# Layer two's short last blocks, loads in the arms of missing blocks, and an accumulator for the third block

## The chip, the core and the metric

The kernel runs on one core of a Trainium2 chip. The time is the device time of one execution in microseconds; three runs of the kernel before took 1007.67, 1007.77 and 1010.33 us, the median is 1007.77. The engines are TensorE (matrix products), VectorE, ScalarE, GpSimd and SyncE (SP), which issues most DMAs. In the profile PE is TensorE's products, PEld its weight loads, DVE is VectorE, ACT is ScalarE, POOL is GpSimd.

## The reference

Attention over 4 x 8 heads of 576 x 64, in which each query keeps its 32 best keys, gives 2304 tokens of 512 values. Two mixture layers of 8 experts follow. Each sends a token to the one expert that its gate rates highest; the second computes only tokens whose skip score is positive and adds its result to the token.

```python
for e in range(E):                      # layer two; xc are the tokens with x @ w_skip > 0
    mask = e_idx == e
    h = np.maximum(xc[mask] @ w1[e], 0.0)          # [rows, 512] @ [512, 1024]
    y[mask] = gate_w[mask, None] * (h @ w2[e])     # [rows, 1024] @ [1024, 512]
out[do_compute] = xc + y
```

With the inputs timed, layer one's experts get 416, 213, 291, 369, 216, 215, 285 and 299 rows, layer two's 177, 156, 141, 117, 320, 314, 175 and 143.

## The kernel before

The attention fills the first 480 us and scatters each token's row into its expert's stretch of a table in DRAM. Then come 16 experts, eight a layer, one after the other, with their order of work written out by hand (the program is scheduled as it is written). Every engine takes its instructions in that order.

Numbers are kept as pairs: a value is split into a high half (rounded to the format that TensorE multiplies at full pace, F32R) and a low half (the rest). A product is then high x high, high x low and low x high. Weights come by DMA into one of eight raw buffers (`fetch`); `split` (L779) lets ScalarE copy the high half and GpSimd or VectorE subtract it for the low one, and then fetches the raw data of eight pieces later. `post.lo` (`LO`) says which of an expert's eight pieces VectorE subtracts: 1, 3 and 5 in layer two. VectorE's `one_port` (L82) is an elementwise operation that also accumulates into a spare column.

An expert (`expert`, L879) does this:

- `xT` (L822): the tokens, up to `BLOCKS` blocks of 128 rows (four in layer one, three in layer two), are transposed by TensorE and split. The first two blocks always run; `optional` (L807) puts the others inside `If`s on the number of rows.
- For each f of 0 to 7, `mm1` (L832) multiplies the first weights by all tokens at once, 12 products into one of three accumulators H. Two nested `If`s on TensorE choose the smallest of four widths that holds the rows: (192, 256, 320, 384) in layer two. ScalarE and VectorE make h's halves from it, 384 columns wide. In between the weights of this expert's second product and the next expert's first are split.
- `mm2` (L861) multiplies h of a block of 128 rows by the second weights: 24 products of 512 columns into an accumulator, eight f by three pairs. First the third and fourth blocks, inside `If`s, then block 1 into Y[1], then block 0 into Y[0]; of block 0 the last three f come after the next expert's transposes. A third block takes Y[0], a fourth one of H.
- `post` makes a block's result. `later` gives its further steps: in layer two the scatter to the output, in layer one also transposes (`turn`), products (`logits`) and counts (`places`) on TensorE that route the token in layer two. `tick` (L873) runs one waiting step of each open block at fixed points between products; those of a third or fourth block again inside `If`s (L932).

An `If` whose arm isn't taken leaves an engine's semaphore behind those of the taken arm. The program then makes it up at the join: the engine's sequencer waits until the engine has done all its instructions, and adds what is missing. In the profile these are EVENT_SEMAPHORE rows of line 813.

The wait that the third block's accumulator brings follows from the order: the products of block 0 write Y[0], and so come behind the third block's read of it on VectorE, also where that block is missing and VectorE only makes up its count.

Of the kernel before, what the change touches and what calls it, by code (L numbers as in the profile page):

```python
# [540 lines left out]
WIDTHS = ((224, 304, 416, 512), (192, 256, 320, 384))  # L541
# [191 lines left out]
class Moe:  # L733
# [9 lines left out]
    def open(self, sb, psum, posts):  # L743
# [5 lines left out]
        self.HT = [sb.tile([128, 2, 512], F32R, name="h%d" % i) for i in range(8)]  # L749
# [48 lines left out]
    def counts(self, e):  # L798

        why = "a count of rows; it is only compared"  # L800
        at = self.ns[0:1, 9 + e:10 + e]
        nc = self.tc.nc
        self.n[e] = (nc.values_load(at, min_val=0, max_val=2304, skip_runtime_bounds_check_because=why),
                     nc.values_load(at, engines=[mybir.EngineType.PE], min_val=0, max_val=2304,
                                    skip_runtime_bounds_check_because=why))

    def optional(self, g, fn, rising=False):  # L807

        n = self.n[g % 8][0]

        def some(j):
            if j < BLOCKS[g // 8]:
                with self.tc.If(n > 128 * j):  # L813
                    if rising:
                        fn(j)
                    some(j + 1)
                    if not rising:
                        fn(j)

        some(2)  # L820
# [51 lines left out]

    def tick(self):  # L873

        for steps in self.open_rows:
            steps.pop(0)()
        self.open_rows = [r for r in self.open_rows if r]

    def expert(self, g):  # L879
# [9 lines left out]
        self.optional(g, lambda j: self.xT(g, j), True)  # L889
# [16 lines left out]
        for f in range(8):  # L906
            self.mm1(g, f)
            for i in range(4):
# [8 lines left out]
            if f == 4 and nxt:  # L917
                self.counts(e + 1)
        if g == 15:
            self.tc.nc.gpsimd.drain()  # L920
        while first:
            first.pop(0)()
        steps = {}

        def block(j):
            p = self.H[(8 * g + 8) % 3] if j == 3 else self.Y[0]
# [4 lines left out]
        late = max(len(t) for t in steps.values())  # L931
        self.open_rows.append([lambda i=i: self.optional(g, lambda j: steps[j][i]())  # L932
                               for i in ((0, 2, 5) if late > 1 else (0,))])
# [11 lines left out]
    def layer(self, layer, ns):  # L945
        tc, nc = self.tc, self.tc.nc
        g0 = layer * 8
        self.ns, self.n, self.open_rows = ns, {}, []
# [7 lines left out]
        self.counts(0)  # L956
# [161 lines left out]
def attention_moe_kernel(ctx: ExitStack, tc, q, k, v, wg1, w11, w12, wskip, wg2, w21, w22, out):  # L1118
# [23 lines left out]
    for bp in range(NP):  # L1142
        nc.gpsimd.iota(ev.tok[:, bp * 9:bp * 9 + 8], pattern=[[S, 2], [128, 4]], base=2 * bp * S, channel_multiplier=1,
                       allow_small_or_imprecise_dtypes=True)
        for b in range(2):
            nc.gpsimd.iota(ev.tok[b * 64:b * 64 + 64, bp * 9 + 8:bp * 9 + 9], pattern=[[0, 1]],
                           base=(2 * bp + b) * S + 512, channel_multiplier=1, allow_small_or_imprecise_dtypes=True)
    ev.wrong = consts.tile([128, 3], F32, name="wrong")
# [101 lines left out]
```

## Time and profile before

| | us |
|---|---|
| median of three runs | 1007.77 |
| the profiled execution | 1005.58 |
| its span, first to last instruction | 1003.8 |
| TensorE's products busy in the span | 875.3 |
| VectorE, ScalarE, GpSimd busy | 719.7, 672.6, 631.8 |
| layer one's first product starts at | 482.7 |
| layer two's first transposes start at | 783.9 |

The profile is of one execution. Busy time is the union of an engine's instructions; products overlap one another in the records, so that the distance between two starts is the better price of one. "Idle before" is the time in which an engine had nothing running, with what released it.

### The profile page before, as it was taken

To read this page: it belongs to the slowest core of one execution; us is meant where nothing else is said; L and a number is where in the kernel's file an instruction comes from. 1 tells how busy PE (TensorE), PEld (TensorE's weight loads), DVE (VectorE), ACT (ScalarE), POOL (GpSimd) and SP (SyncE) were. 2 spreads that over 40 slices of the span, in tenths; PEclk is the share of its full clock that TensorE was granted. 3 is DMA by queue.
4 is the path that set the end of the run, shared out by engine and by line. 5 is a ranking of instruction groups with operands and counts; after the bars stand their busy time and mean duration, and the time that the engine had idled before them with its cause. 6 is when DMAs were issued, how large, how long until landed. Compare 5 with 4: busy or idle time off the path is not lost. (4 is left out here: it accounts for less than half of the span.)

```text
span 1003.8 us, 20600 instructions
## 1 busy us (share of the span) xinstructions
PE 875.3 (87%) x6343; PEld 695.5 (69%) x6343; DVE 719.7 (72%) x3411; ACT 672.6 (67%) x1342; POOL 631.8 (63%) x446
## 2 busy tenths in 40 slices
PE   7678888778778878778999999999998899999997
PEld 5355555455545555556988988887887788889886
DVE  7999999999999999997336634644563456654362
ACT  6699999999989999984535534555452444443342
POOL 6878878877879999853226435444543666654464
PEclk9599999999999999999999999999999999999999
DMA  6897010010202000002836534555533566665530
GB/s 227 262 314 238 24 49 25 3 71 2 72 1 93 13 33 32 2 1 97 287 114 214 175 132 150 176 191 192 168 121 99 185 209 213 219 197 163 183 115 27
DMA packets 55033, 127.72 MB, mean 127 GB/s; under 512 B 8105, under 2 KB 8105, under 8 KB 54864
## 3 DMA queue, kind: packets, MB, share of 16 engines
q1 hardware_dynamic: 46208, 107.64, 33.4%
q0 software_dynamic: 6400, 12.65, 3.3%
q10 hardware_dynamic: 2256, 5.25, 1.5%
q8 instruction: 97, 1.59, 0.7%
q14 instruction: 72, 0.59, 0.2%
HBM read 96.04 MB, written 37.86 MB: 133 GB/s over the span
## 5 line engine op out<-in xcount | busy, mean ns | idle before, releaser
L788 POOL TENSOR_TENSOR w<-raw,w 128x1024 fp32r<-128x1024 f32 x72 | 174.7, 2439 | 185.5 <-ACT w L786 116.6
L867 PE MATMUL y<-w,h 128*128 128x512 f32 x936 | 228.4, 396 | 10.6 <-PEq L813 4.1
L240 POOL TENSOR_TENSOR y<-s,sg 128x576 f32<-128x576 f32 x144 | 204.3, 1440 | 41.8 <-ACT sg L237 32.6
L843 PE MATMUL hp<-xT,w 128*128 128x192 f32 (+4 forms) x1536 | 212.2, 296 | 3.3 <-DVE h L858 2.4
L867 PEld LDWEIGHTS y<-w,h 128*128 128x128 f32 x936 | 171.4, 188 | 53.6 <-issue 13.7
L843 PEld LDWEIGHTS hp<-xT,w 128*128 128x128 f32 x1536 | 203.3, 190 | 6.3 <-DVE h L858 3.8
L209 DVE MAX8 ca<-s 128x8 f32<-128x82 f32 (+1 forms) x1008 | 154.2, 228 | 4.8 <-ACT s L198 4.8
L286 POOL TENSOR_TENSOR r<-s,r 128x576 f32<-128x576 f32 x96 | 135.9, 1429 | 19.4 <-DVE r L282 15.1
L858 DVE SCALAR_TENSOR_TENSOR h<-hp,h 128x512 fp32r<-128x512 f32 (+1 forms) x128 | 77.9, 621 | 79.8 <-ACT h L857 79.7
L857 ACT ACTIVATE h<-hp 128x512 fp32r<-128x512 f32 (+1 forms) x128 | 69.8, 545 | 93.5 <-PE hp L843 87.3
L786 ACT ACTIVATE w<-raw 128x1024 fp32r<-128x1024 f32 x126 | 131.4, 1054 | 0.9 <-POOL w L788 0.5
L322 PE MATMUL m<-ident,p 128*128 128x128 f32 x576 | 95.2, 292 | 29.7 <-DVE whole L362 11.2
L788 DVE TENSOR_TENSOR w<-raw,w 128x1024 fp32r<-128x1024 f32 x54 | 99.3, 1839 | 24.5 <-ACTq L813 15.2
L237 ACT ACTIVATE sg<-s,tm 128x576 f32<-128x576 f32 x144 | 112.0, 797 | 6.5 <-POOL tm L228 5.9
L322 PEld LDWEIGHTS m<-ident,p 128*128 128x128 f32 x576 | 64.7, 145 | 68.9 <-ACT p L294 21.6
L247 DVE MAX8 my<-y 128x8 f32<-128x576 f32 x144 | 101.9, 747 | 2.3 <-POOL y L240 2.3
L109 PE MATMUL s<-kT,qT 64*128 64x288 f32 x512 | 84.4, 448 | 15.2 <-ACT s L198 7.5
L198 ACT ACTIVATE s<-s 128x1152 f32<-128x1152 f32 (+1 forms) x73 | 81.5, 1118 | 12.1 <-PE s L109 9.6
L150 PE MATMUL m<-pT,v 128*64 128x128 f32 (+1 forms) x1280 | 85.5, 277 | 0.7 <-ACT oT L339 0.4
L328 ACT ACTIVATE pT<-m 128x512 f32<-128x512 f32 x144 | 80.5, 609 | 5.6 <-PE m L322 5.6
L294 ACT ACTIVATE p<-r,neg 128x576 f32<-128x576 f32 x96 | 75.4, 787 | 6.8 <-POOL r L286 6.4
L630 POOL DMA_INDIRECT out_dram<-yo,ix x40 | 50.0, 1249 | 41.8 <-DVE yo L1110 24.1
(166 smaller groups left out, 1217.3 us busy)
## 6 DMA issues: line engine op xcount, KB each, us to landing
raw<-in_moe_w_dram SPq DMA_DIRECT2D x119, 512.0 KB, 4.5
x<-zrow SPq DMA_DIRECT2D x16, 1028.0 KB, 18.8
xg<-x SPq DMA_DIRECT2D x50, 257.0 KB, 3.6
v<-in_v_dram SPq DMA_DIRECT2D x8, 576.0 KB, 4.0
kT<-in_k_dram SPq DMA_DIRECT2D x7, 576.0 KB, 3.9
qT<-in_q_dram SPq DMA_DIRECT2D x7, 576.0 KB, 4.8
raw<-in_moe_w_dram ACTq DMA_DIRECT2D x7, 512.0 KB, 6.4
xg<-x ACTq DMA_DIRECT2D x6, 257.0 KB, 4.9
```

Source lines behind the costliest of these rows:

```text
L109: nc.tensor.matmul(p[:, c, :288], d["qT"][h, b, t * 128:t * 128 + 128], d["kT"][h, b, cs], start=True, stop=True)
L150: nc.tensor.matmul(po[i * 64:i * 64 + 64, cs], d["vt"][:, b, i, c] if c < 4 else d["v8"][i * 64:i * 64 + 64, b], pts[i][:, c, cs] if c < 4 ...
L209: nc.vector.max(out=ca[:, c], in_=e["s"][hh][:, cut[c]:cut[c + 1]])
L237: nc.scalar.activation(sg, e["s"][hh], AF.Sign, bias=bt["tm"][:, w:w + 1], scale=-ONE_BELOW, accum_out=bt["ac"][:, w:w + 1])
L240: nc.gpsimd.tensor_mul(y, e["s"][hh], sg)
L247: nc.vector.max(out=bt["my"][:, 2 * i + hh, 8:], in_=e["y"][hh])
L286: nc.gpsimd.tensor_tensor(r, e["s"][hh], r, op=OP.subtract)
L322: nc.tensor.transpose(pp[:, c], e["p"][:, hh, c * 128:c * 128 + 128], ident)
L786: nc.scalar.activation(t[:, 0], raw, AF.Copy)
L788: eng.tensor_tensor(t[:, 1], raw, t[:, 0].bitcast(F32), op=OP.subtract)
L843: nc.tensor.matmul(p[:, :W], self.w1(g, c)[:, a, fs], x[:, c, b, :W], start=(i == 0), stop=(i == 11))
L867: nc.tensor.matmul(p, self.HT[f][:, a, js], self.W2[f // 2][:, b, f % 2 * 512:f % 2 * 512 + 512], start=(f + a + b == 0), stop=(f == 7 and ...
```

## The change

In layer two, mm1's widths become three: 192, 320, 384. All eight h tiles are now slices of two larger ones. VectorE also loads an expert's number of rows into a register.

`beside`: after f = 3 and f = 7 of the first product, if the last block of the expert has at most 64 rows, VectorE copies the low half of h of these rows into the 64 columns behind their high half, for four f at once. One load of 128 columns then carries both halves of such a block.

`seconds` takes the place of the loop over `mm2` in layer two. `mm2s` does a block's high half against both halves of the weights, in an order that leaves f = 4 to 7 against the low weights for last; then an `If` on TensorE: a full block does these four and the eight of h's low half; a short block does these four, each cut into two of 256 columns (the last on 64 rows), and four products of 16 columns with zeros. ScalarE copies the lower 64 rows of the accumulator into `low`. `finish` adds them to the upper 64 rows by a product with a shifted identity (`down`), or, where the block is full or missing, loads a weight of zeros. Block 1 is finished after two f of block 0, a third block at the tick in the middle of block 1.

A third block gets an accumulator of H, in both layers. And in the arms of missing blocks TensorE loads 16 columns of ones as many times as the taken arm has products: with the transposes (4 a block, both layers) and layer one's later steps (4, 4 and 2 a block).

```diff
-WIDTHS = ((224, 304, 416, 512), (192, 256, 320, 384))
+WIDTHS = ((224, 304, 416, 512), (192, 320, 384))
...
-        self.HT = [sb.tile([128, 2, 512], F32R, name="h%d" % i) for i in range(8)]
+        self.HH = [sb.tile([128, 4, 2, 512], F32R, name="h%d" % i) for i in range(2)]
+        self.HT = [h[:, i] for h in self.HH for i in range(4)]
+        self.low = [sb.tile([128, 512], F32R, name="low%d" % i) for i in range(2)]
...
+        if layer:
+            self.short[e] = nc.values_load(at, engines=[mybir.EngineType.DVE], min_val=0, max_val=2304,
+                                           skip_runtime_bounds_check_because=why)
+    def beside(self, e, half):
+        n, h = self.short[e], self.HH[half]
+        def move(j):
+            at = 128 * j
+            one_port(self.tc, self.ev, h[:, :, 0, at + 64:at + 128], h[:, :, 1, at:at + 64].bitcast(F32), 1.0, OP.mult)
+        with self.tc.If(n <= 192) as c:
+            move(1)
+        with c.Else():
+            with self.tc.If(n > 256):
+                with self.tc.If(n <= 320):
+                    move(2)
-    def optional(self, g, fn, rising=False):
+    def optional(self, g, fn, rising=False, products=0):
...
-                with self.tc.If(n > 128 * j):
+                with self.tc.If(n > 128 * j) as c:
...
+                if products:
+                    with c.Else():
+                        for i in range(products * (BLOCKS[g // 8] - j)):
+                            self.tc.nc.tensor.ldweights(self.ev.ones[:, :16])
...
+    def part(self, e, j):
+        return self.H[(8 * e + 9) % 3] if j == 2 else self.Y[j]
+    def mm2s(self, e, j, fs=range(8), ticks=True):
...
+        def product(f, a, b, last, rows=slice(0, 128), cut=1):
+            for i in range(cut):
+                c = slice(i * 512 // cut, (i + 1) * 512 // cut)
+                nc.tensor.matmul(p[rows, c], self.HT[f][:, a, js][:, rows],
+                                 self.W2[f // 2][:, b, f % 2 * 512 + c.start:f % 2 * 512 + c.stop],
+                                 start=(f + a + b == 0), stop=last)
+        for f in fs:
+            for b in range(2 if f < 4 else 1):
+                product(f, 0, b, False)
+            if ticks and f == 3:
+                self.tick()
+        with self.tc.If(self.n[e][1] > 128 * j + 64) as c:
+            for f in range(4, 8):
+                product(f, 0, 1, False)
+            for f in fs:
+                product(f, 1, 0, f == 7)
+        with c.Else():
+            for f in range(4, 8):
+                product(f, 0, 1, False, slice(0, 128 if f < 7 else 64), 2)
+            for i in range(4):
+                nc.tensor.matmul(p[64:, :16], self.ev.none, self.ev.ones[:, :16], start=False, stop=i == 3)
+        nc.scalar.activation(self.low[j % 2][64:], p[64:], AF.Copy)
+        if ticks:
+            self.tick()
+        return p
+    def finish(self, e, j):
+        pe, n, p = self.tc.nc.tensor, self.n[e][1], self.part(e, j)
+        def add():
+            pe.matmul(p[:64], self.ev.down[64:], self.low[j % 2][64:], start=False, stop=True)
+        with self.tc.If(n > 128 * j + 64) as c:
+            pe.ldweights(self.ev.none)
+        with c.Else():
+            if j == 1:
+                add()
...
+    def seconds(self, g):
+        e, post, steps = g % 8, self.posts[1], {}
+        def block(j):
+            self.mm2s(e, j, ticks=False)
+            steps[j] = post.later(g, j)
+        self.optional(g, block)
+        self.open_rows.append([lambda: (self.finish(e, 2), self.optional(
+            g, lambda j: (post(g, j, self.XG[g % 2][j], self.part(e, j)), steps[j][0]())))])
+        self.split(8 * g + 10, post.lo)
+        self.mm2s(e, 1)
+        self.split(8 * g + 11, post.lo)
+        self.mm2(0, range(2), False)
+        self.finish(e, 1)
+        post(g, 1, self.XG[g % 2][1], self.Y[1])
+        self.open_rows.append(post.later(g, 1))
+        self.mm2(0, range(2, HF if e < 7 else 8))
...
-        self.optional(g, lambda j: self.xT(g, j), True)
+        self.optional(g, lambda j: self.xT(g, j), True, 4)
...
+            if layer and f % 4 == 3:
+                self.beside(e, f // 4)
...
+        if layer:
+            return self.seconds(g)
...
-            p = self.H[(8 * g + 8) % 3] if j == 3 else self.Y[0]
+            p = self.H[(8 * g + 11 - j) % 3]
...
-        late = max(len(t) for t in steps.values())
-        self.open_rows.append([lambda i=i: self.optional(g, lambda j: steps[j][i]())
-                               for i in ((0, 2, 5) if late > 1 else (0,))])
+        self.open_rows.append([lambda i=i, n=n: self.optional(g, lambda j: steps[j][i](), products=n)
+                               for i, n in ((0, 4), (2, 4), (5, 2))])
```

## Rows read from the trace of the kernel before

**Rows 1.** The page: busy us by engine; GpSimd's busy tenths in 40 slices.

```profile
PE 875.3 (87%) x6343; PEld 695.5 (69%) x6343; DVE 719.7 (72%) x3411; ACT 672.6 (67%) x1342; POOL 631.8 (63%) x446
...
POOL 6878878877879999853226435444543666654464
```

**Rows 2.** Busy time by engine in two stretches: layer one, layer two.

```profile
core 0: us, PE busy (x) PEld busy (x) DVE busy (x) ACT busy (x) POOL busy (x), PEclk, DMA share, GB/s
526.00:783.00 257.00, 243.56 (x1498) 212.53 (x1498) 129.74 (x452) 124.70 (x207) 121.00 (x71) 0.99 0.49 161
...
783.00:998.00 215.00, 205.94 (x1278) 182.35 (x1278) 111.83 (x142) 95.28 (x142) 120.91 (x55) 1.00 0.54 172
```

**Rows 3.** TensorE's timeline, layer two: start, length, line, operation, count [idle before].

```profile
858.10 1.04 PE L827 MATMUL m<-ident,xg 128*128 128x128 f32 x8
...
861.45 6.84 PE L843 MATMUL hp<-xT,w 128*128 128x192 f32 x60
...
872.91 5.70 PE L867 MATMUL y<-w,h 128*128 128x512 f32 x24
879.52 3.71 PE L867 MATMUL y<-w,h 128*128 128x512 f32 x15 [0.91 <-DVEq L813]
883.06 1.48 PE L827 MATMUL m<-ident,xg 128*128 128x128 f32 x12
...
886.44 14.24 PE L843 MATMUL hp<-xT,w 128*128 128x320 f32 x96
900.51 14.47 PE L867 MATMUL y<-w,h 128*128 128x512 f32 x63
```

**Rows 4.** Line 813 from 526 us: TensorE's sequencer events, length in ns.

```profile
L813 PEldq EVENT_SEMAPHORE  x46: 51/51/51, 542.4 to 986.3; - x46
```

**Rows 5.** TensorE's timeline, layer one: second, third and eighth expert.

```profile
542.51 2.99 PE L867 MATMUL y<-w,h 128*128 128x512 f32 x12
545.64 2.98 PE L867 MATMUL y<-w,h 128*128 128x512 f32 x12
...
553.22 1.47 PE L827 MATMUL m<-ident,xg 128*128 128x128 f32 x12
555.12 2.34 PE L867 MATMUL y<-w,h 128*128 128x512 f32 x9 [0.42 <-PEq L813]
...
759.38 3.00 PE L867 MATMUL y<-w,h 128*128 128x512 f32 x12
762.68 1.03 PE L1070 MATMUL m<-wgt,yT 128*128 128x9 f32 x8 [0.30 <-PEq L813]
```

**Rows 6.** TensorE's timeline, layer one: a pair of small products.

```profile
740.59 0.18 PE L610 MATMUL m<-ob,tri 128*128 128x8 bf16 x1
740.62 0.17 PE L611 MATMUL m<-ob,ones 128*128 128x8 bf16 x1
```

**Rows 7.** Timeline of the other engines in layer two, fourth expert's second product.

```profile
868.85 9.46 POOL L788 TENSOR_TENSOR w<-raw,w 128x1024 fp32r<-128x1024 f32 x4
...
873.18 2.96 ACT L786 ACTIVATE w<-raw 128x1024 fp32r<-128x1024 f32 x3
...
874.27 5.14 DVE L788 TENSOR_TENSOR w<-raw,w 128x1024 fp32r<-128x1024 f32 x1 [0.39 <-ACT w L786]
...
880.55 1.22 DVE L788 TENSOR_TENSOR w<-raw,w 128x1024 fp32r<-128x1024 f32 x1
```

**Rows 8.** Line 84 (`one_port`): length in ns, least, median and most.

```profile
L84 DVE TENSOR_SCALAR_CACHE_REDUCE kb<-kths x24: 153/160/163, 34.1 to 451.7; 128x6 f32<-128x6 f32 x24
```

**Rows 9.** Groups by line and form: busy us, mean ns of one.

```profile
L282 DVE TENSOR_SCALAR r<-s,kths 128x576 f32<-128x576 f32 x43 | 26.8, 624 | 0.0
...
L1065 ACT ACTIVATE yT<-m 128x512 f32<-128x512 f32 x22 | 13.0, 596 | 31.6 <-PE m L1064 31.6
```

**Rows 10.** TensorE's waits, 783 to 1004 us: total us, times, longest.

```profile
PE y L867 <- DVEq L813: 2.1, 3, 0.9
...
PE y L867 <- PEq L813: 1.5, 3, 1.2
...
PE y L867 <- issue: 1.2, 1, 1.2
```

## What I predicted

> **What bounds the kernel now.** I read the page first: TensorE is busy 87% of the span [rows 1]. The busy time by stage says more. From 526 to 783 us (layer one after its first expert) TensorE's products take 243.6 of 257 us, from 783 to 998 (layer two) 205.9 of 215, at a granted clock of 0.99 and 1.00, that is 2.4 GHz; no other engine is over 57% there, and DMA is at about half [rows 2]. So both layers are a row of products on TensorE, and the change is worth what it takes off that row. TensorE's timeline gives the prices. Products of 512 columns: 63 take 14.47 us and 24 take 5.70, so (14.47-5.70)/39 = 0.225 us apiece. Products of 320 columns (the row from 886.44): 14.24/96 = 0.148; of 192: 6.84/60 = 0.114 [rows 3]. From 512 to 320 that is 0.0004 us a column, but 192 columns lie above that line, so there the weight load in front of each product sets the pace, at about 0.11.
>
> **Missing blocks' arms.** Where a block is missing, TensorE's sequencer makes up its semaphore count with an event that waits until all products are done; there are 46 of these from 526 us on [rows 4]. Twelve products should take 2.70 us; with such an arm between them the next one starts 3.13 us after the first (0.43 late), and where the arm is followed by another block's transposes or logits 3.30 us (0.60 late) [rows 5]. In layer one seven of eight experts lack a block, and each has three such arms behind its tokens' steps: 7 x (0.43+0.43+0.60) = 10.2 us. The arm in front of the first product: with all three blocks of layer two there, 12 transposes and 9 products take 886.44-883.06 = 3.38 us, with a block missing 8 transposes and the 9 take 861.45-858.10 = 3.35 [rows 3]; four transposes at 0.11 are 0.43, so the arm costs 0.40. In layer one with one block missing, 12 transposes (1.32) are followed by the product only after 1.90: 0.58 [rows 5]. Three experts at 0.40 and four at 0.58 make 3.5, six of layer two 2.4. Gross: 16.1 us in 34 arms. The arms around the blocks' own products stay.
>
> What stands there instead is 164 loads of 16 columns: layer one 40 with the transposes and 100 with the steps, layer two 24. The trace has no such load alone. The nearest: two loads of 128 bf16 columns, each with a product of 8 columns, start 0.03 us apart [rows 6]. I take 0.03 a load, and 0.11 an arm for the next large load, which then stands in the open: 0.23 for four, 0.35 for eight, 0.17 for two. That is 4 x 0.63 + 3 x 0.93 for the steps, 4 x 0.23 + 3 x 0.35 for layer one's transposes, 6 x 0.23 in layer two: 8.7 us. **Net: 7.4 off.** Bounds: nothing, if all of it lies in the shadow of the running product (16.1 off); and 0.11 a load as for a large one, with 0.11 an arm: 164 x 0.11 + 34 x 0.11 = 21.8, which is 5.7 lost. I stay near the pair, the only small loads in the trace.
>
> On this the Trainium skill has a price (TensorE: Matmul & The Clock Gate, section "LDWEIGHTS (loading the stationary operand)"): a load takes its columns over 1.2 ns, whatever the rows. For 16 columns that would be an estimate of 0.013 us, 2.1 us for all in place of 4.9, and the forecast 2.8 lower (the next large load's 0.11 left as it is). No row here shows a load of 16 columns.
>
> **Short last block.** All eight experts of layer two have a last block of at most 64 rows (177, 156, 141, 117, 320, 314, 175 and 143 rows), so each takes the short arm once. Before: 24 products of 512 columns, 5.40. After: 12 of these (2.70), 8 of 256 columns (0.122 by the slope above: 0.98), four of 16 columns with a weight of zeros (as the small pairs, 0.12 and 0.11 behind them), and later one product of 512 columns that adds the lower half (0.225): 4.13. Saved 1.27, **eight times: 10.2.** The branch is new, but the first product's branches, two ahead of each group of 12, cost nothing that its row of 60 products shows (6.84/60, the pace of the loads). Each expert also runs one load in place of an addition it doesn't need: 8 x 0.14 = 1.1 lost.
>
> What the short block adds off TensorE: ScalarE copies half a bank per block (512 columns out of PSUM take it 0.60 [rows 9]). The copy waits for TensorE behind two splits, and the third split behind it moves from 2.2 to about 4.9 us after the block's start at 872.91; all three are over 3.2 after that start now [rows 7]. Behind that split stand VectorE's half of it and the block's result: done near 8.6 after the start, just ahead of the next tokens' transposed rows. The fetch that the split issues on SP goes 3 us later; its data are used an expert later. The addition comes six products (1.35) after the block, the copy is done about 0.8 after it: hidden with 0.5 to spare; with ScalarE late, TensorE waits for the difference. VectorE gets two moves of 256 elements an expert. By the row of 576 elements in 0.62 us that is 0.28 [rows 9], and by the 6-element row of the same operation with accumulator 0.16 [rows 8] and the other 250 elements at that pace 0.43; 0.3 to 0.5 with the accumulator's read. The first lies between two results of the first product, whose buffers have a group of products to spare. The second ends about 1.7 us after the last group of the first product; TensorE wants it after eight products, 1.8. I take 0.06 a block for a late one, 0.5 lost, between nothing and 0.3 a block. Queued behind the move is VectorE's split, for which TensorE doesn't wait before the next expert.
>
> **Third block's accumulator.** The products of the first block, which come last, wait for VectorE now: the missing third block would have used their accumulator, and VectorE gets to that arm only after a split that took 5.14 us instead of 1.22 [rows 7]: the next 15 products start at 879.52 instead of 878.31, 1.21 late of which 0.91 is idle [rows 3]. There are three such waits, 2.1 us idle [rows 10], and with about 0.3 of restart each 3.0. With its own buffer nothing there waits for that arm; the first group of the next expert uses this buffer some 10 us later. **3.0 off**; nothing, if another wait for the same queue takes its place. Beside it stand two single stalls of 1.2 at the same place in the first two experts, put down to TensorE's own sequencer and to issue [rows 10]. Their cause isn't shown; I count half: 1.2 (between 0 and 2.4).
>
> **Three widths.** The eight experts take 192 or 320 columns before and after, so the products stay. One branch fewer in 48 groups: nothing, since none of these branches shows in the row. In layer one the third block's other buffer frees nothing that a row shows.
>
> **Sum:** 7.4 + 10.2 - 1.1 - 0.5 + 3.0 + 1.2 = 20.2 us. Of the profiled execution's 1005.58 (span 1003.8 and 1.8 around it) 985.4 remain; the median of the runs, 1007.77, is 2.2 above that execution, so I forecast **987.5**.
>
> **The rivals.** *Loads as dear as the drain.* If a small load costs what a large one does, the arms lose 5.7 instead of gaining 7.4: 1001. For it: no load of theirs has a product to hide behind; against it: the pair 0.03 apart [rows 6]. *Loads hidden.* The other bound: 8.7 less, 979. For it: products of 512 columns go at 0.225, their own length, so the load of each lies beside the product before [rows 3]; against it: only one load can lie there for each product. *The wait moves.* TensorE still waits for VectorE's arm, or for ScalarE's copy of the half bank: the 4.2 of the accumulator are gone and 0.5 an expert is added: 996. For it: VectorE's split stays where it is, and ScalarE's order now has a wait for TensorE in it.
>
> *Slower: the moves wait for GpSimd.* VectorE's split of two SBUF inputs took 5.14 instead of 1.22 while GpSimd ran four splits without a gap, 9.46 us from 868.85 [rows 7]. If the moves are held in the same way, the first one keeps the later results back until two of these are over (4.8 us, of which 3.5 reach TensorE after its spare group), and the second holds the short block's fifth group for up to 4: 7 us in each of the six experts of two blocks, 42 in all, so 987.5 + 42 = 1029. It turns the sign from 20.2/6 = 3.4 us an expert on. Against it: 24 operations of this very form, in a stage where GpSimd is busy six to nine tenths, never took over 0.163 [rows 1, 8]. The Trainium skill has this as a rule (SBUF — State Buffer, section "SBUF: two separate sides"): VectorE and GpSimd share a port pair under an exclusive lock, taken by VectorE's two-port modes and its operations with two SBUF inputs. The split agrees with it, 5.14; the moves have one input and an accumulator, and by the rule would wait only if they ran in such a mode.
>
> **Chances.** The forecast 56% (982 to 992), loads dear 13%, loads hidden 13%, the wait moved 11%, the moves held 4%, and 3% that these gains are eaten by something I don't see. The range goes from 977 to 999: the hidden loads with the two single stalls gone below, most of the dear loads above. A measurement here tells 0.3%, 3 us, from no change. Only the held moves and half of the unseen end above that: faster 0.92, same 0.03, slower 0.05.
>
> **What would show it.** The events in TensorE's sequencer fall from 46 to about 13. The packs of 12 products with an arm between start about 2.9 apart. A short block, up to the next product, takes near 3.9 in place of 5.4, and an expert of two blocks 22.6 in place of 25.0. VectorE's moves last 0.3 to 0.5 each. VectorE's name disappears from TensorE's waits before the second product. I am wrong if an arm with loads takes as long as before, if a move lasts over 1 us, or if TensorE waits before the addition.

## The result: 2.3% faster, 1 us below the forecast

The changed kernel takes 986.51 us (median of 5 runs, 983.11 to 987.18) beside 1008.55 of the kernel before on the same chip (1007.67 to 1011.57): a ratio of 0.977, interval 0.975 to 0.979. Forecast were 987.5, between 977 and 999. Its profiled execution took 984.61, the span is 982.8; before it was 1003.8.

TensorE's timeline, cut at the first transposes of each expert, says where the 21.0 us of the span went. Times are us:

| stretch | before | after | difference | forecast |
|---|---|---|---|---|
| up to the first expert | 478.3 | 478.6 | +0.3 | 0 |
| layer one, first expert | 46.45 | 46.46 | 0 | 0 |
| layer one, experts 2 to 8 | 259.10 | 248.85 | -10.25 | -6.4 |
| layer two | 219.94 | 208.88 | -11.06 | -13.8 |

So the total came out right although two terms were wrong: layer one gave 3.9 more than forecast and layer two 2.7 less. That these nearly cancel is luck. (Forecast for layer one: 10.2 + 3.5 for the drains, less 40 and 100 loads with their restarts, 7.3; the other terms are layer two's.)

**Profile after: the missing blocks' arms.** This is TensorE's timeline of layer one's second expert, the answer to [rows 5], and the sequencer's events at the branches, the answer to [rows 4] (line 834 is the `If` of `optional`, 868 and 892 are the two products, 852 the transposes, 1178 the logits).

```profile
542.57 8.54 PE L892 MATMUL y<-w,h 128*128 128x512 f32 x36
550.94 0.60 PE L1172 MATMUL m<-ident,yo 128*128 128x128 f32 x4
551.30 0.94 PE L892 MATMUL y<-w,h 128*128 128x512 f32 x3
552.08 1.47 PE L852 MATMUL m<-ident,xg 128*128 128x128 f32 x12
553.35 2.35 PE L892 MATMUL y<-w,h 128*128 128x512 f32 x9
555.53 0.95 PE L1178 MATMUL m<-wgt,yT 128*128 128x9 f32 x8
...
L834 PEldq EVENT_SEMAPHORE  x13: 51/51/51, 542.5 to 966.1; - x13
```

Before, three groups of 12 products started 3.13 apart and the next transposes at 552.06, 9.55 after the first; now all 36 are one row, and the transposes come 8.37 after its start: 1.18 of the forecast's gross 1.46 (0.43 + 0.43 + 0.60) came back. The twelve transposes and nine products up to the logits take 3.45, where they took 4.08. The events fell from 46 to 13, the number forecast. The weight loads in that row:

```profile
545.15 0.19 PEld L843 LDWEIGHTS <-ones 128*16 128x16 bf16 x8
545.27 2.62 PEld L892 LDWEIGHTS y<-w,h 128*128 128x128 f32 x12
547.93 0.19 PEld L843 LDWEIGHTS <-ones 128*16 128x16 bf16 x8
548.05 1.00 PEld L892 LDWEIGHTS y<-w,h 128*128 128x128 f32 x5
```

Eight small loads occupy 0.12 (545.15 to 545.27), 0.015 each, beside the product that runs then. By the Trainium skill (TensorE: Matmul & The Clock Gate, section "LDWEIGHTS (loading the stationary operand)") an estimate for 16 columns is 0.013; the trace's 0.015 is near it.

**Profile after: layer two's first expert.** TensorE's timeline, which answers to [rows 3] (911 and 929 the short block's products and zeros, 940 the addition):

```profile
788.41 3.95 PE L911 MATMUL y<-w,h 128*128 128x512 f32 x20
792.29 0.29 PE L929 MATMUL y<-ones,none 128*64 128x16 bf16 x4
792.51 1.66 PE L892 MATMUL y<-w,h 128*128 128x512 f32 x6
794.11 0.44 PE L940 MATMUL y<-low,down 64*64 64x512 f32 x1
794.48 2.36 PE L892 MATMUL y<-w,h 128*128 128x512 f32 x9
796.67 1.03 PE L852 MATMUL m<-ident,xg 128*128 128x128 f32 x8
797.50 2.35 PE L892 MATMUL y<-w,h 128*128 128x512 f32 x9
799.69 3.49 PE L868 MATMUL hp<-xT,w 128*128 128x192 f32 x30
```

The short block with its zeros takes 4.10 up to the next product (3.90 forecast without the addition). The six products, the addition and the start behind it take 1.97, where six alone are 6 x 0.225 = 1.35, so 0.62 more. Start by start, 0.11 of this stands behind the first of the six, which follows the zeros (0.339 to the second), and 0.11 more behind the product after the addition (0.342). So the addition costs near 0.6, not 0.225. TensorE is not idle ahead of it, and ScalarE's copy was done at 793.21, 0.9 earlier: it is hidden. Transposes and nine products: 799.69 - 796.67 = 3.02 instead of 3.35 (0.33 off; 0.40 - 0.23 forecast).

VectorE's moves (line 84: length in ns, least, median and most), then the one at 807.23 and GpSimd beside it, the answers to [rows 7, 8]:

```profile
L84 DVE TENSOR_SCALAR_CACHE_REDUCE h<-h x16: 420/420/422, 784.4 to 967.2; 128x256 fp32r<-128x256 f32 x16
...
807.23 0.42 DVE L84 TENSOR_SCALAR_CACHE_REDUCE h<-h 128x256 fp32r<-128x256 f32 x1
...
807.16 9.45 POOL L790 TENSOR_TENSOR w<-raw,w 128x1024 fp32r<-128x1024 f32 x4
```

All sixteen took 0.42, near the higher of the two values worked out (0.28 and 0.43), also the one that started 0.07 us into GpSimd's 9.45. The rival in which GpSimd holds them is out. The Trainium skill (SBUF — State Buffer, section "SBUF: two separate sides") lets an operation with one SBUF input wait for the shared port only in a two-port mode; the trace agrees, by 0.42 beside GpSimd as without it.

TensorE's waits in layer two, the answer to [rows 10]:

```profile
PE m L852 <- DMA xg<-x: 2.3, 2, 2.0
PE hp L868 <- DVE h L883: 1.5, 6, 0.3
PE m L852 <- DVE awi L474: 1.1, 1, 1.1
PE hp L868 <- DVEq L834: 0.4, 1, 0.4
```

Gone are VectorE's three waits before the second product, and both single stalls. New is one of 1.1 for `awi`, the flag that every engine reads behind layer two's third expert: TensorE's sequencer now reaches its register load before VectorE has written the flag. TensorE restarts 0.56 after that write.

In layer one's sixth expert TensorE stands 1.33 idle before the last group of the first product, 0.45 before. The lines are VectorE's results of the first product, TensorE's branch that chooses this group's width (shortest, median and longest of two, in ns) and the group itself, then the first and the third in the kernel before, and last the stretch behind it (columns as in [rows 2]):

```profile
671.10 1.88 DVE L883 SCALAR_TENSOR_TENSOR h<-hp,h 128x512 fp32r<-128x512 f32 x3
L875 PEldq COMPARE_BRANCH  x2: 208/709/1210, 671.2 to 672.5; - x2
672.78 2.19 PE L868 MATMUL hp<-xT,w 128*128 128x224 f32 x12 [1.33 <-DVE h L883]
...
678.68 1.88 DVE L858 SCALAR_TENSOR_TENSOR h<-hp,h 128x512 fp32r<-128x512 f32 x3
679.47 1.60 PE L843 MATMUL hp<-xT,w 128*128 128x224 f32 x12 [0.45 <-DVE h L858]
...
673.60:677.00 3.40, 3.25 (x12) 2.62 (x12) 1.17 (x3) 1.82 (x3) 2.94 (x3) 0.50 0.39 132
```

The profile names VectorE's result both times. Each VectorE line is three results (x3) of 0.68. The group needs the first of them, since it writes the accumulator which that one reads. Before, the group starts 0.11 after this result's end (679.36 and 679.47): a wait for VectorE. Now it starts 1.00 after (671.78 and 672.78): VectorE had long been done, and what fills that time is the branch, which lasted 1.21 from 671.24 on where the median is 0.21. Behind the group's start the granted clock is 0.50, the lower of its two levels of 1.2 and 2.4 GHz. That expert alone is 0.9 longer than before (29.40 and 28.51), where experts with as many blocks gained 1.5 to 1.9 and take 27.0. More on such branches stands in the last section.

### The profile page after: what moved, and what is told of

Read it like the earlier page. It is cut to its first block, busy times and chain, and to the rows that moved or that the text cites. A ratio compares the mean times of both kernels' runs of the same rounds, so it can differ in the third digit from the quotient of the medians.

```text
span 982.8 us, 20872 instructions
## 1 busy us (share of the span) xinstructions
PE 867.1 (88%) x6351; PEld 695.0 (71%) x6523; DVE 726.1 (74%) x3444; ACT 680.0 (69%) x1353; POOL 623.8 (63%) x446
## 3 DMA queue, kind: packets, MB, share of 16 engines
q8 instruction: 94, 1.54, 0.6%
## 5 line engine op out<-in xcount | busy, mean ns | idle before, releaser
L868 PE MATMUL hp<-xT,w 128*128 128x192 f32 (+4 forms) x1536 | 212.9, 296 | 4.6 <-DVE h L883 3.6
L892 PE MATMUL y<-w,h 128*128 128x512 f32 x576 | 146.7, 402 | 0.4
L892 PEld LDWEIGHTS y<-w,h 128*128 128x128 f32 x576 | 104.8, 189 | 22.6 <-issue 2.4
L109 PE MATMUL s<-kT,qT 64*128 64x288 f32 x512 | 86.5, 458 | 14.4 <-ACT s L198 7.5
L198 ACT ACTIVATE s<-s 128x1152 f32<-128x1152 f32 (+1 forms) x73 | 81.5, 1118 | 14.3 <-PE s L109 10.3
L150 PEld LDWEIGHTS m<-pT,v 128*64 128x64 f32 x1280 | 68.6, 145 | 14.5 <-ACT pT L328 4.6
```

Of the source, the lines that this page charges most:

```text
L109: nc.tensor.matmul(p[:, c, :288], d["qT"][h, b, t * 128:t * 128 + 128], d["kT"][h, b, cs], start=True, stop=True)
L150: nc.tensor.matmul(po[i * 64:i * 64 + 64, cs], d["vt"][:, b, i, c] if c < 4 else d["v8"][i * 64:i * 64 + 64, b], pts[i][:, c, cs] if c < 4 ...
L868: nc.tensor.matmul(p[:, :W], self.w1(g, c)[:, a, fs], x[:, c, b, :W], start=(i == 0), stop=(i == 11))
L892: nc.tensor.matmul(p, self.HT[f][:, a, js], self.W2[f // 2][:, b, f % 2 * 512:f % 2 * 512 + 512], start=(f + a + b == 0), stop=(f == 7 and ...
```

## The experiments

Eleven kernels, three batches, each on one chip beside the kernel before. Whole times of one chip differ by a few us with the part ahead of the experts (attention, 478 to 486 us), so the stages of the profiles are compared as well. "Layer one" is without its first expert.

| kernel | us | ratio [interval] | layer one | layer two | events |
|---|---|---|---|---|---|
| before | 1008.55 | 1 | 259.1 | 219.9 | 46 |
| changed | 986.51 | 0.977 [0.975, 0.979] | 248.9 | 208.9 | 13 |
| e1 arms alone | 1003.95 | 0.991 [0.988, 0.993] | 248.5 | 219.8 | 13 |
| e2 accumulator alone | 1011.82 | 0.999 [0.997, 1.001] | 259.4 | 217.0 | 47 |
| e3 no short blocks | 997.58 | 0.984 [0.980, 0.988] | 249.2 | 215.0 | 13 |
| e4 loads tripled | 997.31 | 0.985 [0.981, 0.990] | 251.7 | 209.6 | 13 |
| e5 whole addition | 988.71 | 0.975 [0.972, 0.977] | 247.0 | 207.2 | 13 |
| e6 products uncut | 990.61 | 0.976 [0.974, 0.978] | 249.4 | 209.2 | 13 |
| e7 splits (1, 3) | 994.27 | 0.981 [0.978, 0.983] | 247.3 | 212.9 | 13 |
| e8 three widths alone | 1011.59 | 0.998 [0.997, 0.999] | 258.9 | 218.8 | 47 |
| e9 changed again | 991.30 | 0.978 [0.977, 0.980] | 248.6 | 208.9 | 13 |
| e10 addition and flag | 988.25 | 0.974 [0.972, 0.976] | 250.0 | 207.1 | 13 |
| e11 and block arms | 990.33 | 0.979 [0.976, 0.981] | 252.0 | 204.5 | 0 |

The medians of the kernel before were 1012.77 beside e1 to e4, 1013.11 beside e5 to e8, 1013.26 beside e9 to e11. Its events are 47 too with one at 525.8 us, just ahead of the stretch of [rows 4]. There is one profile of each kernel.

**e1: the kernel before, with only the loads in the missing blocks' arms.**

```diff
-    def optional(self, g, fn, rising=False):
+    def optional(self, g, fn, rising=False, products=0):
...
+                if products:
+                    with c.Else():
+                        for i in range(products * (BLOCKS[g // 8] - j)):
+                            self.tc.nc.tensor.ldweights(self.ev.ones[:, :16])
...
-        self.optional(g, lambda j: self.xT(g, j), True)
+        self.optional(g, lambda j: self.xT(g, j), True, 4)
...
```

> The kernel before with the small loads in the missing blocks' arms alone (both layers). Theory A (the two traces: packs of 12 products now follow one another without a gap, eight loads starting in 0.12 us beside a product that runs 0.23): the drains of 34 arms come back nearly whole, about 14 us off, ratio to before near 0.986; sequencer events of TensorE at the arms' line from 46 to 13. Theory B (the prediction's price of 0.03 a load and 0.11 an arm): 7.4 off, ratio 0.993. Theory C (what was won in layer one is given back to VectorE's waits): under 5 off.

Layer one falls by 10.6, all that the change gives there. Layer two as a whole gives nothing (-0.2). Its fourth, seventh and eighth experts are 0.33 to 0.36 shorter, so the transposes' arms do come back there. But the two single stalls stand in the second and third expert now, not in the first and second, and are 2.0 and 1.7 long instead of 1.2 each: the first expert is 0.9 shorter, these two together 1.7 longer. VectorE's waits did not grow (1.2, before 2.1). The waits, columns as in [rows 10]:

```profile
PE y L871 <- PEq L813: 3.7, 2, 2.0
...
PE y L871 <- DVEq L813: 1.2, 2, 0.9
```

Theory A holds in layer one; the whole time, 0.991, lies between it and Theory B.

**e2: the kernel before, with only the third block's own accumulator.**

```diff
-            p = self.H[(8 * g + 8) % 3] if j == 3 else self.Y[0]
+            p = self.H[(8 * g + 11 - j) % 3]
```

> The kernel before with a third block's own accumulator alone. Theory A: the three waits of block 0's products for VectorE's arm go, 3.0 us; the two single stalls of 1.2 us beside them are the same kind of wait and go too: 5.4 off, ratio 0.9946. Theory B: the single stalls have another cause and stay, 3.0 off, ratio 0.997. Theory C: another wait for the same queue takes the place, nothing off.

Theory B holds. Layer two is 3.0 shorter, the forecast's term; 2.9 of it lie in the third, fourth and seventh experts, where VectorE's waits before the second product stood and are gone. One single stall of 1.6 stays, in the second expert. The whole time can't tell 3 us here (the interval holds 1), the stage can.

**e3: the changed kernel, its short blocks computed in full.**

```diff
-        with self.tc.If(self.n[e][1] > 128 * j + 64) as c:
+        with self.tc.If(self.n[e][1] > 0) as c:
...
-        with self.tc.If(n > 128 * j + 64) as c:
+        with self.tc.If(n > 0) as c:
```

> The changed kernel with its full arm always taken: every last block of layer two does 24 products of 512 columns, no product is cut and no half is added; the moves and the copies of half a bank stay. Theory A (the changed trace: the addition costs 0.58 with what it does to its neighbours, the four small products 0.42): the short arm is worth 0.7 us a block, so 5.5 us slower than the changed kernel, ratio to before near 0.983. Theory B (the prediction's prices): 1.27 a block, 10.2 slower, ratio 0.988.

Layer two is 6.1 longer, 0.76 a block. TensorE's timeline of the first expert says the same:

```profile
795.68 5.71 PE L911 MATMUL y<-w,h 128*128 128x512 f32 x24
801.23 3.59 PE L892 MATMUL y<-w,h 128*128 128x512 f32 x15
804.66 1.03 PE L852 MATMUL m<-ident,xg 128*128 128x128 f32 x8
```

From the block's start to the transposes it is 8.98; in the changed kernel 796.67 - 788.41 = 8.26. A short block is worth 0.72, not 1.27.

**e4: the changed kernel with two further loads for each one, in missing and present blocks' arms alike (512 more).**

```diff
+                    for i in range(2 * products):
+                        self.tc.nc.tensor.ldweights(self.ev.ones[:, :16])
...
-                        for i in range(products * (BLOCKS[g // 8] - j)):
+                        for i in range(3 * products * (BLOCKS[g // 8] - j)):
```

> The changed kernel with three times the small loads in the arms of missing blocks, and as many more in the taken arms that the counts stay equal: 512 loads more. Theory A (loads start 0.0155 us apart and lie beside the running product up to seven or eight of them): what exceeds the shadow is 0.0155 each, about 4 us slower than the changed kernel. Theory B (0.03 each in the open): 15 us slower. Theory C (any number is hidden): no difference.

The 456 more loads outside layer one's first expert cost 3.6 us (2.9 and 0.7), 0.008 each; Theory A holds. The 2.9 would be more, had the sixth expert not gone without the lower clock here (28.6 where the changed kernel takes 29.4). An arm of 24 loads where there were 8 shows why (TensorE's loads in layer one's second expert):

```profile
549.58 0.19 PEld L894 LDWEIGHTS y<-w,h 128*128 128x128 f32 x1
549.81 0.43 PEld L845 LDWEIGHTS <-ones 128*16 128x16 bf16 x24
550.17 0.30 PEld L894 LDWEIGHTS y<-w,h 128*128 128x128 f32 x2
```

24 loads are 0.36, 0.015 each. The products around them start 0.368 and then 0.338 apart instead of 0.227 each, 0.25 more together, which is 16 or 17 loads; the other seven or eight lie beside the running product. With eight loads, in the changed kernel, the products stand 0.232 apart: all hidden. In layer two, where the arm follows transposes of 128 columns, eight loads more cost about 0.12 in most experts, 0.015 each: there none is hidden.

**e5: the changed kernel, its addition over all 128 rows (the upper ones zero).**

```diff
+        for t in self.low:
+            self.tc.nc.scalar.activation(t[:64], self.ev.zrow[:64, :512], AF.Copy)
...
-            pe.matmul(p[:64], self.ev.down[64:], self.low[j % 2][64:], start=False, stop=True)
+            pe.matmul(p[:64], self.ev.down, self.low[j % 2], start=False, stop=True)
```

> The changed kernel with the addition of the lower half over all 128 rows (the upper 64 rows of its weight and of its data are zeros) in place of the lower 64. Theory A: what makes the addition cost 0.58 us instead of a product's 0.225 is that it uses a quarter of the array, so that neither its own weight load nor the next one runs beside a product; over 128 rows about 0.3 a block comes back, 2.5 us off the changed kernel in layer two. Theory B: it is the 64 columns of the weight, which stay; nothing comes back.

The experts that no single wait touches are 0.35 shorter (22.41 and 22.76, second expert), so the addition loses nearly all of its surplus. In the timeline of the fourth expert of layer two:

```profile
866.99 1.66 PE L894 MATMUL y<-w,h 128*128 128x512 f32 x6
868.49 0.40 PE L942 MATMUL y<-low,down 128*64 128x512 f32 x1
868.73 2.22 PE L894 MATMUL y<-w,h 128*128 128x512 f32 x9
870.79 1.47 PE L854 MATMUL m<-ident,xg 128*128 128x128 f32 x12
```

From the six products to the transposes it is 3.80, in the changed kernel (first expert) 796.67 - 792.51 = 4.16. Counted from start to start, less the products around it, the addition takes 0.58 there and 0.25 here. So its 64 rows were dear, not the 64 columns of its weight, which stay; Theory A holds. The weight loads show where the time goes, first in the changed kernel, then here:

```profile
794.11 0.13 PEld L940 LDWEIGHTS y<-low,down 64*64 64x64 f32 x1 [0.37 <-issue]
794.47 0.30 PEld L892 LDWEIGHTS y<-w,h 128*128 128x128 f32 x2 [0.24 <-issue]
...
868.25 0.14 PEld L942 LDWEIGHTS y<-low,down 128*64 128x64 f32 x1
```

The load of the 64x64 product starts with that product (794.11), and the next load with the next product: neither lies beside the product ahead of it. The load over 128 rows starts at 868.25, with the last of the six products and 0.24 ahead of its own, and lies beside that one.

**e6: the changed kernel with the last four of the short block's products uncut, one zero product and seven small loads.**

```diff
-            for f in range(4, 8):
-                product(f, 0, 1, False, slice(0, 128 if f < 7 else 64), 2)
-            for i in range(4):
-                nc.tensor.matmul(p[64:, :16], self.ev.none, self.ev.ones[:, :16], start=False, stop=i == 3)
+            for f in range(4, 7):
+                product(f, 0, 1, False)
+            product(7, 0, 1, False, slice(0, 64))
+            nc.tensor.matmul(p[64:, :16], self.ev.none, self.ev.ones[:, :16], start=False, stop=True)
+            for i in range(7):
+                nc.tensor.ldweights(self.ev.ones[:, :16])
```

> The changed kernel with the short arm's last four products uncut (512 columns instead of twice 256) and one small product with zeros instead of four; seven loads of 16 columns keep the count. By the changed trace cut products and zeros take 1.38 us a block, of which the switch to the small products and back is 0.2; uncut four take 0.91, one small product with the switch 0.23. Theory A (the prices add up): 0.24 a block, 1.9 us off. Theory B (the cut products hide the last results' wait for VectorE's moves): nothing, or a wait of TensorE at the fifth group.

No difference: the block takes 4.08 up to the next product, cut it took 4.10, and layer two's experts 2 to 7 are equal to 0.03. Theory A is out. So is the reason that Theory B gives: TensorE's waits show none that could have eaten a gain. In its timeline the zero product starts at 799.28 and the next large one at 799.51: 0.23 with the seven loads; in the changed kernel the four zeros take 0.22 up to the next.

```profile
795.43 3.92 PE L911 MATMUL y<-w,h 128*128 128x512 f32 x16
799.28 0.20 PE L929 MATMUL y<-ones,none 128*64 128x16 bf16 x1
799.51 1.66 PE L892 MATMUL y<-w,h 128*128 128x512 f32 x6
```

**e7: the changed kernel with a third of VectorE's splits in layer two given to GpSimd.**

```diff
-LO = ((1, 3, 5, 7), (1, 3, 5))
+LO = ((1, 3, 5, 7), (1, 3))
```

> The changed kernel with piece 5 of layer two's weights subtracted by GpSimd instead of VectorE. Theory A: the stall before the sixth group of the first product (0.42 us in six experts, put down to VectorE's result) comes from that split, which waits 1.1 us for GpSimd's and keeps the results back; without it 2.5 us off in layer two. Theory B: GpSimd then has six pieces of 2.4 us an expert, and its chain makes the later splits late: VectorE's other pieces end some 2.4 us later, the block's result behind them, and TensorE waits for the next tokens' rows, slower by over 1 us an expert.

Slower by 4 us in layer two. The wait for VectorE's `h` at the sixth group (1.5 in all, 0.3 at most) goes, as Theory A had it, and undisturbed experts take 22.3 instead of 22.8; but the total goes Theory B's way. TensorE's waits there, then VectorE's split ahead of the flag:

```profile
PE m L852 <- DMA raw<-in_moe_w_dram: 3.2, 1, 3.2
...
PE hp L868 <- DVEq L834: 1.3, 3, 0.5
...
839.09 7.23 DVE L790 TENSOR_TENSOR w<-raw,w 128x1024 fp32r<-128x1024 f32 x1
```

The 3.2 are put down to a fetch, but they stand at the third expert's flag, and TensorE restarts 0.56 after VectorE wrote it, as in the changed kernel. So it is the flag's wait, 2.1 longer, because VectorE's split ahead of it took 7.23 beside GpSimd instead of 5.15. The same wait of 1.1 bears a fetch's name in e3 and e4.

**e8: the kernel before, with only the three widths.**

```diff
-WIDTHS = ((224, 304, 416, 512), (192, 256, 320, 384))
+WIDTHS = ((224, 304, 416, 512), (192, 320, 384))
```

> The kernel before with three widths in layer two alone. Theory A: the single stalls of 1.2 to 2.0 us at the start of the second product, which appear in the first experts of layer two in the kernel before and in both single edits, and in no kernel with three widths, come with the longer row of unused arms (768 products and loads less an expert's four widths against three): they go, layer two 2.4 us shorter. Theory B: nothing changes; the stalls come from elsewhere.

1.1 off in layer two, 1.0 of it in the first expert. Theory A holds for the stalls and for half of its time: both single stalls are gone from the waits, and VectorE's take part of their place, four times and 3.7 us instead of three times and 2.1 [rows 10]:

```profile
PE y L867 <- DVEq L813: 3.7, 4, 0.9
```

**e9, e10, e11: the changed kernel again; with e5's addition and the flag read two experts later; and with small loads in the arms of the blocks' own products too.**

```diff
     nc.vector.tensor_copy(i, f)
-    return nc.values_load(i[0:1, 0:1], min_val=0, max_val=128)
+    return i
...
-                self.ev.again = anything_wrong(tc, self.ev)
+                wrong = anything_wrong(tc, self.ev)
+            if layer == 1 and e == 4:
+                self.ev.again = tc.nc.values_load(wrong[0:1, 0:1], min_val=0, max_val=128)
```

```diff
-        self.optional(g, block)
+        self.optional(g, block, products=24)
```

> The changed kernel itself, beside its two improvements on one chip. Both theories: 0.974 to 0.978 of the kernel before, layer two 208 to 210 us, and TensorE's wait of 1.1 to 1.4 us for the flag (awi) in front of the transposes of layer two's fourth expert there once. If that wait were chance, it would be gone here.

> The changed kernel with the lower half added by a product over all 128 rows of weights and data (the upper ones zero), and with the flag that all engines read behind layer two's third expert read two experts later. Theory A (the 64x64 product stands in the open, and the wait is TensorE's own register load held by VectorE's place in its queue): 8 x 0.3 = 2.4 us and 1.1 to 1.4 us off the changed kernel, layer two near 205.5 us, no wait with awi in TensorE's list. Theory B (the flag's wait only covers another one, for the fetched rows or for VectorE): the wait appears under another name at the same transposes, layer two near 207.

> The former one, and 24 small weight loads for each missing block also in the arms of the blocks' own products (13 arms in 13 experts, with 24 or 48 loads). Theory A (a join with its drain costs 0.40 us, and 24 loads cost 0.14 beside the running product and 0.11 behind it, as the tripled loads showed): 0.15 off in each of 13 arms, 2.0 us, layer two near 204.5, layer one 0.9 shorter, TensorE's event count down from 15 to about 2. Theory B (the arm's loads stand behind a product that ends a group, so nothing hides them): 24 x 0.0152 + 0.11 = 0.47, as much as the drain; no change within 1 us.

e9 repeats the changed kernel, the flag's wait of 1.1 included. e10 is the fastest kernel beside it: 988.25 and 991.30, 3.1 us less, intervals apart (ends 0.9755 and 0.9766). Theory A holds: layer two's experts 2 to 8 take 182.4 instead of 186.3, the flag's wait is gone, and no other name stands at those transposes. Layer two as a whole shows only 1.7, because in this one profile its first expert is 2.2 longer. The granted clock is 0.50 there, 1.2 GHz, and 95 products in a row take 13.59 where e9's take 11.29:

```profile
783.00:789.70 6.70, 6.50 (x31) 6.05 (x30) 1.25 (x2) 2.10 (x5) 1.50 (x1) 0.50 0.14 51
```

e11 goes for Theory B. TensorE's events are gone, but experts 2 to 8 of layer two take 182.3, as in e10. (The 204.5 for all of layer two, the number of Theory A, comes from the first expert, which has no lower clock here.) The median is 2.1 us above e10's, intervals apart. The products ahead of these arms are 192 or 224 columns, whose own weight loads already set the pace, so nothing hides the small ones: in layer one's second expert 48 of them put 0.74 between two products that stood 0.11 apart (548.08 and 548.82). And a stall of TensorE stands right behind, and makes layer one longer (its timeline; then the DMA queues from 549 to 552 us):

```profile
548.82 0.67 PE L894 MATMUL y<-w,h 128*128 128x512 f32 x1 [0.47 <-issue]
552.63 9.73 PE L894 MATMUL y<-w,h 128*128 128x512 f32 x35 [3.15 <-issue]
...
q8 instruction: 1, 0.02, 2.0%
```

## Why the prediction was right, and where two errors cancelled

| term of the sum | forecast | measured | from |
|---|---|---|---|
| drains less loads, layer one | 6.4 | 12 to 13 in the arms, 10.3 net | e1; 1.8 in the second expert (1.18 + 0.63), times 7 |
| the same, layer two | 1.0 | 2.0 | 6 x 0.33 |
| short block | 10.2 | 5.8 | e3, 8 x 0.72 |
| load in place of an addition | -1.1 | -0.1 | see below |
| late move | -0.5 | 0 | waits after |
| third accumulator | 3.0 | 3.0 | e2 |
| single stalls | 1.2 | 2.4 | rows 10; waits after |
| three widths | 0 | 1.1 alone | e8 |
| not foreseen | 0 | -1.3 flag, -0.3 `h` (1.5 for 1.2 idle), -2.4 layer one's sixth expert | waits after; e10; 29.4 for 27.0 |

**Loads, mis-sized.** The forecast took 0.03 a load from the pair of small products [rows 6] and put every load in the open, with 0.11 an arm behind them. A small load is 0.015, and some eight lie beside a running product of 512 columns. The argument against the rival "loads hidden", that only one load can lie there for each product, was wrong: e4 shows where hiding ends, and e11 that nothing is hidden where products stand 0.11 apart, at the pace of their own loads. So the steps' arms got 1.18 of their 1.46 back, not 0.53. The load in `finish`'s other arm, once an expert, is the same error: a load of 64 columns beside a product of the short block cost 0.01 (790.103 to 790.340 between the products around it, 0.237 for 0.227), not 0.14.

**Short block, mis-sized.** The cut products were right: 20 products start within 3.88, the forecast's 2.70 + 0.98 is 3.68; 0.09 stands at the switch to a bf16 product, 0.1 is spread over the rest. The addition was not: near 0.6 for 0.225, the one step "one product of 512 columns that adds the lower half". It was priced as a product like its neighbours though the trace of before had none with 64 rows. e5 shows that the rows made it dear: over 128 rows it gives 0.36 a block back. The other 0.2 of the missing 0.55 lies at the zeros, 0.09 ahead of them and 0.11 behind, and e6 finds the same cost with one of them as with four.

**Third accumulator, right,** to 0.1 us, and alone (e2). e1 keeps the two terms apart: its seventh expert is 0.36 shorter by the arms, though VectorE's wait of 0.9 still stands in it.

**Single stalls.** Counted at half because their cause wasn't shown; both went. e8 ties them to the widths: with four, they stand in the kernel before, e1 and (one) e2, not always in the same experts; with three, in none of the ten profiles of layer two, e8's included. By time e8 gives 1.1, since VectorE's wait takes the second stall's place there. So the forecast's "three widths: nothing" was the wrong place and "half of two stalls" the wrong size for one and the same thing. What may hold TensorE there is in the last section.

**The rivals.** Loads as dear as the drain is out by 0.015 a load; the moves held by GpSimd by 0.42 sixteen times. The wait moved is out for the place named, but a wait did move: 1.1 to the flag. The measured terms, gains of 13 + 2 + 5.8 + 3 + 2.4 less what was given back (1.3 for the flag, 0.3 for `h`, 2.4 in layer one's sixth expert), make 22; the spans differ by 21.0.

**What the sum had no term for.** In layer one's sixth expert the same stall, idle 1.0 to 1.7, stands in e1, e3 to e7, e9 and e10, each time 0.7 to 1.3 after VectorE's result and behind a branch of 0.9 to 1.5. e11 waits there 0.4, for VectorE. Behind the stall the granted clock went to 0.50 in the changed kernel, e3, e6, e9 and e10, and the expert took 29.4 to 29.7; it did not in e1, e4, e5 and e7, where it took 27.5 to 28.6, nor in e11 (27.4). So most of the loss is the clock's. Why it fell in some of them and not in others is open: the stall was 1.47 in e7 and 1.49 in e9.

## What to carry to other kernels

Price an instruction by one of its own shape: the product with 64 rows cost more than twice the one with 128 rows (0.58 and 0.25), and zeros in the upper half were cheaper than leaving it out. A join that drains an engine can be bought back with dummy work on the same path, and it is free only as far as the running instruction covers it; count what lies ahead of each arm (a 512-column product here covers some eight small loads, a 224-column one none). Before you believe the name that a profile gives to a wait, compare that one's end with the restart: 0.11 apart was a wait for VectorE, 1.00 apart was a branch. When one engine's row is shortened, look for the next reader of a value: the register load of a flag, which TensorE did not wait for before, cost 1.1 as soon as TensorE came earlier, and two experts later it was free again.

## What the runs showed that was not expected

**Long branches end in step with an instruction queue, and TensorE may be waiting for its own code.** The single stalls all follow one packet of 16 KB on an instruction queue (q8). In e11 it ran from 550.26 to 551.23, and TensorE went on at 552.63, 1.4 later; in the kernel before packets ended at 797.46 and 823.17, products restarted at 799.03 and 824.62 (1.6 and 1.5 later); in e1 at 818.51 and 843.40, restarts at 820.04 and 844.97 (1.5 and 1.6); in e2 at 827.30, restart at 828.62 (1.3); and once in layer one, in e1, at 656.77, restart at 658.32 (1.6). The stall of layer one's sixth expert follows a packet that ended at 671.08, by 1.7. TensorE's branch ahead of the restart at 799.03 is one record, in ns:

```profile
L813 PEldq COMPARE_BRANCH  x1: 3153/3153/3153, 795.7 to 795.7; - x1
```

Such records say more than the stalls. From 480 us on, the thirteen traces have 130 branches of TensorE that last over 0.5 us, up to 4.0, where the median is 0.21. All 130 end between 1.29 and 1.54 behind the end of a 16 KB packet on q8; of the 5442 shorter ones 3.5% do. Most of them have no idle time behind them. That fits a sequencer that waits for instructions behind a branch, and e8, where one branch and its unused products less made both stalls vanish (long branches remain in layer two with three widths, without such a stall). It is a pattern in time, though; no run changed the code's place or size alone, so the cause is not shown.

**The zeros cost at their edges.** Between the short block's last fp32r product and the first zero product (bf16) 0.09 more than the pace of the cut ones passes, and 0.11 before the next large one; one such product of 16 columns, with seven small loads, takes 0.23 up to the next large one (e6). The 0.11 more that the first large product then takes to the next (0.339) is not theirs alone: it stands behind the 64x64 addition too (0.342). No run changed the type of the zeros alone.
